# A new order for the seven products of the first matrix product, and one piece of operand work a step

## The chip, the cores and the metric

The kernel runs on one core of one Trainium2 chip, in one launch. A core has a matrix engine (TensorE, PE in the profile; its weight loads are PEld), a vector engine (VectorE, DVE), a scalar engine (ScalarE, ACT), a general engine (GpSimd, POOL) and the queue engine that issues the large transfers (SyncE, SP). Each engine runs its own list of instructions strictly in order and waits at an instruction until what it depends on is done. The metric is the time of one execution on the device in microseconds, and a kernel is told by the median of its runs.

## The reference

Three stages follow each other. Linear attention with a norm gives x of 2304 rows and 512 columns. A mixture of E = 4 dense experts, F = 1024 wide, follows, and then a soft mixture with 8 experts of 4 slots each. The change lies in the second stage:

```
kv  = einsum('bhsd,bhse->bhde', k, v);  out = einsum('bhsd,bhde->bhse', q, kv)
x   = out / sqrt(mean(out*out) + 1e-06) * g_norm        # 2304 x 512
p   = domain_probs / (domain_probs.sum(-1) + 1e-09)
for e in range(4):
    h    = maximum(x @ w1[e], 0)                         # 2304 x 1024, "first product"
    out += p[:, e:e+1] * (h @ w2[e])                     # 2304 x 512,  "second product"
# then: logits = x @ phi, softmax over tokens, slot inputs, 8 small experts, softmax over slots
```

## The kernel before, in words

**Numbers.** Every operand of the two products is kept as a pair of 16-bit numbers, hi (rounded) and lo (what is left), and each product is three matmuls: hi by hi, hi by lo, lo by hi, summed in the same accumulator bank.

**Tiling.** Tokens are cut into five chunks: 0 to 3 have 512 tokens, chunk 4 has 256. Chunks 0 and 1 form the first group, which runs experts 0, 1, 2, 3. Chunks 2, 3 and 4 form the second, which runs experts 3, 2, 1, 0. The first product of one expert and chunk is split into 2 by 2 blocks and done with seven block products P1 to P7 in place of eight (`PROD` names the operand blocks of each: blocks A11 to A22 of the tokens' side with sums S1 to S4, blocks B11 to B22 of the weights' side with sums T1 to T4). Each of them is done for u = 0 and u = 1, two halves of the columns. One such pair (P, u) is a **step**: 12 matmuls of 128x256 (128x128 in chunk 4), by line L890 in `mm1`. So a chunk's first product is 14 steps, in the order of `ORDER` (`ORDER2` in the fast form below): P for u = 0, P for u = 1, and then the next P.

**Banks.** For each u the products add up in three accumulator banks that the code calls x, y and z, and what is needed is a sum up to some point. In the plain form x takes P1, P6, P5, P3 in turn, y takes P2, and z takes P7 and P4. After P1, P6 and P5 the sum in x so far is copied out by ACT (L915); after P2 and P4 DVE adds the bank to such a copy (L918); after P5 it also adds z (L923). A product may not be added to a bank before the engine that reads its state so far is done; that order is kept by semaphores. x comes from a pool of two banks (one for each u), and y and z from another pool of two, so z of u = 0 takes the bank that y of u = 0 had.

**Plain form** (first group, expert 3 of the second group, and chunk 3 of the last expert). What comes out goes through `put`: ACT makes the relu and its hi (L906), and DVE makes lo (L907) one step later. The second product (`mm2`, L955) then reads h.

**Fast form** (experts 2, 1, 0 of the second group, apart from that last chunk). Here the second product is done with seven products too (`mm2_fast`, L991, in the order `ORDER3`), so that h's blocks and their sums S1 to S4 must be made as hi and lo pairs (`fast_h`). After each product ACT copies a bank out (L819 for P1, L821 for P6, L823 for P7), DVE adds a bank to a copy (L825 for P2, L829 for P5, L853 for P3), or ACT takes the relu of P4 (L833). The rest is done in pieces that wait in a list `todo`: the lo of a block (L802), a sum with its hi (L836 and L810 on DVE, with L797 on ACT), and the lo of a sum (L806). `work_off(2)` takes up to two pieces from the front of the list after each step of `mm1`, and `mm2_fast` takes one before each of its steps, or as many as it must until the block that it reads is made.

**Order.** For experts 2 and 1 the list of stages is first(2), first(3), second(2), first(4), second(3), second(4), numbers in brackets being chunks (`FASTSEQ`); for expert 0 it is first(2), first(4), second(2), first(3), second(4), second(3) (`LASTSEQ`). So one first product follows directly on another in one place for each of these three experts. Everything is written out in program order; background work (weights into hi and lo by L601 on ACT and L603 on DVE, sums of weights by L635 on POOL, attention of later chunks, the softmax of the third stage) is spread over the steps by `chain`. In the first chunk, hooks before steps 1, 3, 5, 7 and 9 make the operands that the next products need. For the second group, the weights' blocks of experts 2, 1, 0 are read back from memory in the order that `want_back` lists, on SP's queue.

## Time and profile before

| | |
|---|---|
| median of 3 runs | 870.9 us (870.34 to 871.3) |
| profiled execution | 870.41 us |
| its span, first to last instruction | 868.6 us |
| PE busy | 821.4 us, 95% of the span |
| DVE, ACT, POOL busy | 523.8, 350.6, 96.0 us |
| matmuls of the first product, L890 | 3360, 347.2 us |
| matmuls of the second product, L955 and L991 | 1104 and 1092, 246.1 and 121.0 us |
| mean granted clock of PE | 0.983 |

Each row of a timeline is one run of equal instructions: when it began, how long it took, engine and line, what it writes and reads, how many, and, in brackets, how long the engine had been idle just before and what ended that. "t <- p" means that tile t is written from tile p. Lines are those of the kernel before.

### The profile page before, as it was taken

The page shows a single profiled execution, that of the slowest core. Times are in us where ns is not written, and L with a number is a line of the kernel's source. Part 1 is how long each engine was busy: PE and PEld are TensorE (multiplying, and loading weights), DVE is VectorE, ACT ScalarE, POOL GpSimd, SP SyncE. Part 2 cuts the span into 40 slices and gives each one's busy share as a digit, 9 for nine tenths or more (in the row PEclk, how much of TensorE's full clock was granted, in tenths as well). Part 3 has the DMA queues.
Part 4 walks back from the last instruction along what each step waited for, and adds up shares of the span by engine and source line. Part 5 has one row for each costly group of instructions (what it writes and reads, how often), then busy time and mean ns, then how long its engine had stood idle before and what let it go on. Part 6 is the DMA issues. An engine that isn't in the chain of part 4 may idle for free.

```text
span 868.6 us, 16718 instructions
## 1 busy us (share of the span) xinstructions
PE 821.4 (95%) x7089; PEld 609.2 (70%) x7089; DVE 523.8 (60%) x1002; ACT 350.6 (40%) x681; POOL 96.0 (11%) x69
## 2 busy tenths in 40 slices
PE   8789899999999999999999998999899997999995
PEld 7575748575756676758485687898789887874444
DVE  4788898866895443755844348663876447452414
ACT  2675564553546232635552245222533044231213
POOL 2205622503150400000000000000000000000000
PEclk8799999999999999999999999999999999999998
DMA  8770500295129601125310110135004253079687
GB/s 337 298 267 25 212 31 1 76 356 223 68 86 402 246 1 50 68 79 196 118 54 1 53 46 1 36 136 194 2 1 171 81 204 124 6 268 400 218 350 219
DMA packets 40426, 123.86 MB, mean 143 GB/s; under 512 B 4256, under 2 KB 11296, under 8 KB 40352
## 3 DMA queue, kind: packets, MB, share of 16 engines
q1 hardware_dynamic: 39904, 122.70, 38.5%
q8 instruction: 55, 0.90, 0.4%
q14 instruction: 19, 0.16, 0.1%
q10 hardware_dynamic: 448, 0.10, 0.1%
HBM read 94.47 MB, written 28.31 MB: 141 GB/s over the span
## 4 chain that ended last, share of the span: by engine, by line
PE 68%; DVE 12%; ACT 6%; issue 1%; DMA 0%; SPq 0%; DVEq 0%; ACTq 0%
PE y L955 24%; PE p L890 22%; PE m L991 13%; DVE pages L603 2%; PE s L1578 2%; DVE pages L802 2%; ACT pages L795 1%; PE so L1616 1%; DVE pages L806 1%; PE o L335 1%; ACT t L915 1%; PE x2T L1020 1%; DVE t L810 1%; DVE t L825 1%; PE lg L1043 1%
## 5 line engine op out<-in xcount | busy, mean ns | idle before, releaser
L890 PE MATMUL p<-pages 128*128 128x256 f16 (+1 forms) x3360 | 347.2, 263 | 23.9 <-ACT pages L821 9.8
L890 PEld LDWEIGHTS <-pages 128*128 128x128 f16 x3360 | 302.5, 98 | 63.2 <-issue 29.2
L955 PE MATMUL y<-pages 128*128 128x512 f16 x1104 | 246.1, 379 | 2.5 <-DVE pages L964 2.0
L955 PEld LDWEIGHTS <-pages 128*128 128x128 f16 x1104 | 107.3, 98 | 125.8 <-issue 5.8
L991 PE MATMUL m<-pages 128*128 128x256 f16 x1092 | 121.0, 273 | 2.2 <-DVE pages L1001 2.2
L991 PEld LDWEIGHTS <-pages 128*128 128x128 f16 x1092 | 106.6, 98 | 15.8 <-issue 3.4
L603 DVE SCALAR_TENSOR_TENSOR pages<-pages,s_w 128x512 f16<-128x512 f32 x112 | 100.3, 938 | 5.4 <-ACT pages L601 5.4
L601 ACT ACTIVATE pages<-pages,s_w 128x512 f16<-128x512 f32 x112 | 73.5, 711 | 37.8 <-POOL pages L635 12.0
L915 ACT COPY t<-p 128x512 f32<-128x512 f32 (+1 forms) x72 | 40.0, 562 | 84.0 <-PE p L890 83.9
L906 ACT ACTIVATE pages<-t 128x512 f16<-128x512 f32 (+1 forms) x72 | 44.0, 612 | 71.5 <-DVE t L918 53.2
L1001 DVE SCALAR_TENSOR_TENSOR pages<-m,pc,pages 128x256 f32<-128x256 f32 x91 | 40.8, 481 | 40.7 <-PE m L991 40.6
L907 DVE SCALAR_TENSOR_TENSOR pages<-t,pages 128x512 f16<-128x512 f32 (+1 forms) x72 | 54.6, 761 | 3.0 <-ACT pages L906 0.6
L918 DVE TENSOR_TENSOR t<-p,t 128x512 f32<-128x512 f32 (+1 forms) x48 | 31.7, 664 | 35.2 <-PE p L890 35.2
L635 POOL TENSOR_TENSOR pages<-pages 128x1024 f32<-128x1024 f32 x16 | 40.3, 2521 | 96.6 <-DVE pages L603 62.8
L797 ACT CAST pages<-t 128x512 f16<-128x512 f32 (+1 forms) x48 | 25.5, 538 | 50.9 <-DVE t L810 39.6
L707 POOL TENSOR_TENSOR pages<-pages 128x512 f32<-128x512 f32 x24 | 35.6, 1484 | 81.2 <-DMA pages<-in_w 78.8
L966 DVE SCALAR_TENSOR_TENSOR pages<-y,pc,pages 128x512 f32<-128x512 f32 x28 | 21.0, 749 | 37.8 <-PE y L955 37.8
L1587 POOL MEMSET pages<- 128x1024 f32 x2 | 1.8, 951 | 374.8 <-PE s L1578 374.8
L923 DVE TENSOR_TENSOR t<-p,t 128x512 f32<-128x512 f32 (+1 forms) x24 | 16.1, 669 | 30.7 <-ACT t L915 30.6
L819 ACT COPY t<-p 128x512 f32<-128x512 f32 (+1 forms) x16 | 8.1, 505 | 57.7 <-PE p L890 57.7
L964 DVE TENSOR_SCALAR pages<-y,pc 128x512 f32<-128x512 f32 x18 | 13.4, 747 | 27.8 <-PE y L955 27.8
L795 ACT ACTIVATE pages<-pages 128x512 f16<-128x512 f32 (+1 forms) x32 | 17.2, 546 | 31.5 <-DVE pages L829 19.9
(188 smaller groups left out, 696.5 us busy)
## 6 DMA issues: line engine op xcount, KB each, us to landing
pages<-in_w SPq DMA_DIRECT2D x44, 512.0 KB, 7.9
o<-pages SPq DMA_DIRECT2D x33, 512.0 KB, 9.9
pages<-o SPq DMA_DIRECT2D x33, 512.0 KB, 4.4
pages<-in_m SPq DMA_DIRECT2D x32, 512.0 KB, 5.7
pages<-in_m2a SPq DMA_DIRECT2D x16, 512.0 KB, 6.6
pages<-in_m2b SPq DMA_DIRECT2D x16, 512.0 KB, 10.1
o_t<-pages SPq DMA_DIRECT2D x12, 512.0 KB, 2.8
pages<-o_t SPq DMA_DIRECT2D x12, 512.0 KB, 4.0
```

The costliest lines, as they stand in the source:

```text
L601: nc.scalar.activation(dst[:, 0], src, AF.Copy, scale=s)
L603: nc.vector.scalar_tensor_tensor(out=dst[:, 1], in0=src, scalar=s, in1=dst[:, 0], op0=ALU.mult, op1=ALU.subtract)
L635: self.eng.tensor_tensor(out=self.src(op).ap, in0=a.ap, in1=b.ap, op=ALU.subtract)
L707: eng.tensor_tensor(out=o, in0=a, in1=b, op=ALU.subtract)
L890: nc.tensor.matmul(ps[:, fp * n:fp * n + n], l, r, start=(fp + i == 0 and P in first), stop=(fp == 1 and i == len(mms) - 1 and P in end), ...
L906: nc.scalar.activation(hh, src, AF.Relu)
L907: late.append(lambda: nc.vector.scalar_tensor_tensor(out=hl, in0=src, scalar=0.0, in1=hh, op0=ALU.max, op1=ALU.subtract))
L915: nc.scalar.copy(t, ps)
L918: nc.vector.tensor_tensor(out=t, in0=ps, in1=t, op=ALU.add)
L955: nc.tensor.matmul(ps, a, b, start=(u + kk + fp + i == 0), stop=(u == 1 and kk == 1 and fp == 1 and i == 2))
L991: nc.tensor.matmul(ps, l, r, start=(i == 0 and j == 0 and P in (1, 2, 7)), stop=(i == len(mms) - 1 and j == nh - 1 and P in (2, 3, 4)), sk ...
L1001: nc.vector.scalar_tensor_tensor(out=x, in0=mbank[b][:, 256 * i:256 * i + 256], scalar=pcs[wk[1]][:, t:t + 1], in1=x, op0=ALU.mult, op1=AL ...
```

## The change

`ORDER2` goes, and `ORDER` holds for both forms: P1 P2 P6 P5 P7 P3 P4. The banks are the same in both forms now: x takes P1, P6, P7, P4; y takes P2; z takes P5 and P3. In the plain form P5 (alone in z) is copied by ACT, P7 and P3 are added by DVE, and P4 is the one that `put` reads directly from the bank; before it was P3. In `fast_h` P5 is copied by ACT, P7 and P3 are added by DVE and their hi is made at once (before, A12's hi came as a piece of work), P4's relu comes last, and S1 is made before S2. `work_off` after a step takes one piece, or two while more than 16 wait. The hooks of the first chunk split T1 before step 3 and the pages of T3 before step 5 (before, the other way round), and the read back order is B11, B21, T2, T1, T3, B22, T4.

```
-ORDER = (1, 2, 6, 7, 5, 3, 4)
-ORDER2 = (1, 2, 6, 7, 5, 4, 3)
+ORDER = (1, 2, 6, 5, 7, 3, 4)
...
-        for key in [("o1", o) for o in (B11, B21, T2, T3, T1, T4, B22)] + [
+        for key in [("o1", o) for o in (B11, B21, T2, T1, T3, B22, T4)] + [
...                                                          # fast_h
-        t6, t7, t4 = ([hraw(wk, c, op, v) for v in range(2)] for op in (S4, S1, A12))
+        t6, t5, t4 = ([hraw(wk, c, op, v) for v in range(2)] for op in (S4, S1, S2))
...
-        elif P == 7:
-            nc.scalar.copy(t7[u], ps)
+        elif P == 5:
+            nc.scalar.copy(t5[u], ps)
...
-        elif P == 5:
-            nc.vector.tensor_tensor(out=t7[u], in0=ps, in1=t7[u], op=ALU.add)
-            hi(u, A22, t7[u], True)
-            then(A22, lambda: lo(u, A22, t7[u], True))
-        elif P == 4:
+        elif P == 7:
+            nc.vector.tensor_tensor(out=t5[u], in0=ps, in1=t5[u], op=ALU.add)
+            hi(u, A22, t5[u], True)
+            then(A22, lambda: lo(u, A22, t5[u], True))
+        elif P == 3:
+            nc.vector.tensor_tensor(out=t6[u], in0=ps, in1=t6[u], op=ALU.add)
+            hi(u, A12, t6[u], True)
+            then(A12, lambda: lo(u, A12, t6[u], True))
+        else:
             nc.scalar.activation(t4[u], ps, AF.Relu)
...
+            def first(v, out, op1):
+                nc.vector.scalar_tensor_tensor(out=out[v], in0=t5[v], scalar=0.0, in1=out[v], op0=ALU.max, op1=op1)
...
                 for v in range(2):
-                    then(S2, lambda v=v: comb(v, S2, t1[v], t7[v], ALU.subtract))
+                    then(S1, lambda v=v: first(v, t4, ALU.add))
                 for v in range(2):
-                    then(S1, lambda v=v: comb(v, S1, t4[v], t7[v], ALU.add))
+                    then(S1, lambda v=v: (first(v, t1, ALU.subtract), hi(v, S1, t4[v], False)))
+                for v in range(2):
+                    then(S1, lambda v=v: (lo(v, S1, t4[v], False), hi(v, S2, t1[v], False)))
                 for v in range(2):
                     then(S2, lambda v=v: lo(v, S2, t1[v], False))
-                for v in range(2):
-                    then(S1, lambda v=v: lo(v, S1, t4[v], False))
...                                                          # mm1
-        if fast:
-            b = {1: "x", 6: "x", 7: "x", 4: "x", 2: "y", 5: "z", 3: "z"}[P]
-            first, end = (1, 2, 5), (2, 3, 4)
-        else:
-            b = {1: "x", 6: "x", 5: "x", 3: "x", 2: "y", 7: "z", 4: "z"}[P]
-            first, end = (1, 2, 7), (2, 3, 4)
+        b = {1: "x", 6: "x", 7: "x", 4: "x", 2: "y", 5: "z", 3: "z"}[P]
+        first, end = (1, 2, 5), (2, 3, 4)
...
-            work_off(2)
+            work_off(1 + (len(todo) > 16))
...
-        elif P in (2, 4):
-            t = d[1 if P == 2 else 6]
+        elif P == 4:
+            put(ps, 0, 1)
+        else:
+            t = d[{2: 1, 3: 6, 7: 5}[P]]
             nc.vector.tensor_tensor(out=t, in0=ps, in1=t, op=ALU.add)
-            put(t, 0, int(P == 4))
-        elif P == 3:
-            put(ps, 1, 0)
-        if P == 5:
-            nc.vector.tensor_tensor(out=d[5], in0=d["z"], in1=d[5], op=ALU.add)
-            put(d[5], 1, 1)
+            put(t, int(P != 2), int(P == 7))
...                                                          # hooks before steps 1, 3, 4, 5, 7, 9
-                             lambda: (x_split(2), w_split(T3)), lambda: [f() for f in kv1],
-                             lambda: (w_split(T1), w.t1.release()), lambda: w_split(B22),
+                             lambda: (w_split(T1), w.t1.release()), lambda: [f() for f in kv1],
+                             lambda: (x_split(2), w_split(T3)), lambda: w_split(B22),
```

How the instructions stand now is shown at three places. In these lists p1 is the bank x, p2 is y, p5 or p7 is z, and the numbers behind are group, expert, chunk and u. Lines of the changed kernel are 2 to 8 lower than those of the kernel before.

The first place is ACT in the plain form, chunk 0 of expert 1, from the copies of P6 to the last relu. Before:

```order
L915 COPY t6_0_1_0_0_1399<-p1_0_1_0_0_1321 128x512
L915 COPY t6_0_1_0_1_1415<-p1_0_1_0_1_1338 128x512
L915 COPY t5_0_1_0_0_1458<-p1_0_1_0_0_1321 128x512
L906 ACTIVATE pages_78<-t5_0_1_0_0_1458 128x2x256
L601 ACTIVATE pages_78<-pages_78,s_w2_0_544 128x512
L915 COPY t5_0_1_0_1_1480<-p1_0_1_0_1_1338 128x512
L906 ACTIVATE pages_78<-t5_0_1_0_1_1480 128x2x256
L601 ACTIVATE pages_78<-pages_78,s_w2_0_544 128x512
L906 ACTIVATE pages_78<-p1_0_1_0_0_1321 128x2x256
L906 ACTIVATE pages_78<-p1_0_1_0_1_1338 128x2x256
L906 ACTIVATE pages_78<-t6_0_1_0_0_1399 128x2x256
L906 ACTIVATE pages_78<-t6_0_1_0_1_1415 128x2x256
```

Now:

```order
L910 COPY t6_0_1_0_0_1399<-p1_0_1_0_0_1321 128x512
L910 COPY t6_0_1_0_1_1415<-p1_0_1_0_1_1338 128x512
L910 COPY t5_0_1_0_0_1431<-p5_0_1_0_0_1418 128x512
L910 COPY t5_0_1_0_1_1448<-p5_0_1_0_1_1435 128x512
L901 ACTIVATE pages_78<-t5_0_1_0_0_1431 128x2x256
L599 ACTIVATE pages_78<-pages_78,s_w2_0_548 128x512
L901 ACTIVATE pages_78<-t5_0_1_0_1_1448 128x2x256
L599 ACTIVATE pages_78<-pages_78,s_w2_0_548 128x512
L901 ACTIVATE pages_78<-t6_0_1_0_0_1399 128x2x256
L901 ACTIVATE pages_78<-t6_0_1_0_1_1415 128x2x256
L901 ACTIVATE pages_78<-p1_0_1_0_0_1321 128x2x256
L901 ACTIVATE pages_78<-p1_0_1_0_1_1338 128x2x256
```

The two copies of t5 read z and stand directly behind those of t6, ahead of any relu of t5; before, each read x and had a relu and a weight split (L601) ahead of the second. The relus that read a bank directly (p1) moved from the middle to the end.

The second place is DVE in the fast form, chunk 2 of expert 2, from the first sum for A22 on. Before:

```order
L829 TENSOR_TENSOR pages_78<-p5_1_2_2_0_5086,pages_78 128x512
L802 SCALAR_TENSOR_TENSOR pages_78<-pages_78 128x512
L829 TENSOR_TENSOR pages_78<-p5_1_2_2_1_5102,pages_78 128x512
L802 SCALAR_TENSOR_TENSOR pages_78<-pages_78 128x512
L836 SCALAR_TENSOR_TENSOR t1_1_2_2_0_4985<-t1_1_2_2_0_4985,pages_78 128x512
L836 SCALAR_TENSOR_TENSOR t1_1_2_2_1_5000<-t1_1_2_2_1_5000,pages_78 128x512
L806 TENSOR_TENSOR pages_78<-t1_1_2_2_0_4985,pages_78 128x512
L853 TENSOR_TENSOR pages_78<-p5_1_2_2_0_5086,pages_78 128x512
```

Now:

```order
L827 TENSOR_TENSOR pages_78<-p1_1_2_2_0_4972,pages_78 128x512
L800 SCALAR_TENSOR_TENSOR pages_78<-pages_78 128x512
L827 TENSOR_TENSOR pages_78<-p1_1_2_2_1_4987,pages_78 128x512
L800 SCALAR_TENSOR_TENSOR pages_78<-pages_78 128x512
L831 TENSOR_TENSOR pages_78<-p5_1_2_2_0_5060,pages_78 128x512
L800 SCALAR_TENSOR_TENSOR pages_78<-pages_78 128x512
L831 TENSOR_TENSOR pages_78<-p5_1_2_2_1_5074,pages_78 128x512
L800 SCALAR_TENSOR_TENSOR pages_78<-pages_78 128x512
L838 SCALAR_TENSOR_TENSOR t1_1_2_2_0_4985<-t1_1_2_2_0_4985,pages_78 128x512
L838 SCALAR_TENSOR_TENSOR t1_1_2_2_1_5000<-t1_1_2_2_1_5000,pages_78 128x512
L804 TENSOR_TENSOR pages_78<-t1_1_2_2_0_4985,pages_78 128x512
```

Before, the sums for A22 (L829) alternate with their lo (L802), and the sums for A12 (L853) come after the first sums for S3 (L836). Now the sums for A22 (L827) and those for A12 (L831) both alternate with the lo of the same block (L800), and the sums for S3 (L838) come behind all four.

The same chunk on ACT, from the copies of P6 to the first copies of the next chunk. Before:

```order
L821 COPY pages_78<-p1_1_2_2_0_4972 128x512
L821 COPY pages_78<-p1_1_2_2_1_4987 128x512
L823 COPY pages_78<-p1_1_2_2_0_4972 128x512
L823 COPY pages_78<-p1_1_2_2_1_4987 128x512
L795 ACTIVATE pages_78<-pages_78 128x512 x2
L833 ACTIVATE pages_78<-p1_1_2_2_0_4972 128x512
L797 CAST pages_78<-t1_1_2_2_0_4985 128x512
L833 ACTIVATE pages_78<-p1_1_2_2_1_4987 128x512
L797 CAST pages_78<-t1_1_2_2_1_5000 128x512
```

Now:

```order
L819 COPY pages_78<-p1_1_2_2_0_4972 128x512
L819 COPY pages_78<-p1_1_2_2_1_4987 128x512
L821 COPY pages_78<-p5_1_2_2_0_5060 128x512
L821 COPY pages_78<-p5_1_2_2_1_5074 128x512
L793 ACTIVATE pages_78<-pages_78 128x512 x4
L835 ACTIVATE pages_78<-p1_1_2_2_0_4972 128x512
L795 CAST pages_78<-t1_1_2_2_0_4985 128x512
L835 ACTIVATE pages_78<-p1_1_2_2_1_4987 128x512
L795 CAST pages_78<-t1_1_2_2_1_5000 128x512
L817 COPY t1_1_2_3_0_5191<-p1_1_2_3_0_5178 128x512
```

Before, two relus for hi (L795) stand ahead of P4's relus (L833) and two casts for S2 follow them. Now four stand ahead of P4's relus (L835), and the next chunk's copies of P1 (L817) follow one cast later.

The third place is DVE in the last expert, from the start of chunk 4's second product. Before:

```order
L1001 SCALAR_TENSOR_TENSOR pages_78<-m1_1_0_4_8221,pc_0_549,pages_78 128x256
L1158 TENSOR_REDUCE sc2_8237<-ce2_8127 128x4
L1159 TENSOR_SCALAR sc2_8237<-sc2_8237 128x4
L1160 RECIPROCAL sc2_8237<-sc2_8237 128x4
L1161 TENSOR_TENSOR ce2_8127<-ce2_8127,sc2_8237 128x128
L1001 SCALAR_TENSOR_TENSOR pages_78<-m7_1_0_4_8242,pc_0_549,pages_78 128x256
L1168 TENSOR_SCALAR c4_2_8256<-ce2_8127 128x4x32
L1169 SCALAR_TENSOR_TENSOR c4_2_8256<-ce2_8127,c4_2_8256 128x4x32
L1172 COPY c4_2_8256<-c4_2_8256 128x4x64
L1001 SCALAR_TENSOR_TENSOR pages_78<-m1_1_0_4_8221,pc_0_549,pages_78 128x256
L1127 SCALAR_TENSOR_TENSOR sacc_96<-sacc_96,al2_8107,sp2_8273 128x512
```

Now:

```order
L804 TENSOR_TENSOR pages_78<-pages_78 128x256
L993 SCALAR_TENSOR_TENSOR pages_78<-m1_1_0_4_8213,pc_0_553,pages_78 128x256
L1150 TENSOR_REDUCE sc2_8229<-ce2_8119 128x4
L1151 TENSOR_SCALAR sc2_8229<-sc2_8229 128x4
L1152 RECIPROCAL sc2_8229<-sc2_8229 128x4
L1153 TENSOR_TENSOR ce2_8119<-ce2_8119,sc2_8229 128x128
L804 TENSOR_TENSOR pages_78<-t1_1_0_4_0_7510,pages_78 128x256
L993 SCALAR_TENSOR_TENSOR pages_78<-m7_1_0_4_8235,pc_0_553,pages_78 128x256
L1160 TENSOR_SCALAR c4_2_8249<-ce2_8119 128x4x32
L1161 SCALAR_TENSOR_TENSOR c4_2_8249<-ce2_8119,c4_2_8249 128x4x32
L1164 COPY c4_2_8249<-c4_2_8249 128x4x64
L804 TENSOR_TENSOR pages_78<-t1_1_0_4_1_7531,pages_78 128x256
```

Seven pieces of chunk 4 are left in the list when its second product begins (three of them are the L804 here, two L808 and two L804 follow); before there were none.

## Rows read from the trace of the kernel before

**Rows 1.** Waits of PE, whole span: who waited for whom; us in total, times, longest.
```profile
PE p L890 <- ACT pages L821: 9.8, 8, 2.2
PE p L890 <- ACT t L915: 5.7, 6, 1.9
```

**Rows 2.** Timeline of PE, 50 to 150 us: start, us, line, count, [idle before].
```profile
56.82 1.47 PE L890 MATMUL p<-pages 128*128 128x256 f16 x12 [1.92 <-ACT t L915]
...
101.72 1.47 PE L890 MATMUL p<-pages 128*128 128x256 f16 x12 [1.41 <-ACT t L915]
104.19 4.09 PE L890 MATMUL p<-pages 128*128 128x256 f16 x36 [1.00 <-ACT t L915]
...
120.64 1.46 PE L955 MATMUL y<-pages 128*128 128x512 f16 x6 [2.00 <-DVE pages L964]
```

**Rows 3.** Timeline of DVE, 95 to 125 us.
```profile
101.70 0.69 DVE L923 TENSOR_TENSOR t<-p,t 128x512 f32<-128x512 f32 x1 [0.33 <-ACT t L915]
...
104.17 0.69 DVE L923 TENSOR_TENSOR t<-p,t 128x512 f32<-128x512 f32 x1 [1.12 <-ACT t L915]
...
119.84 0.74 DVE L964 TENSOR_SCALAR pages<-y,pc 128x512 f32<-128x512 f32 x1
```

**Rows 4.** Timeline of PE, 490 to 572 us (expert 2, second group).
```profile
499.24 23.95 PE L890 MATMUL p<-pages 128*128 128x256 f16 x216
523.50 2.78 PE L890 MATMUL p<-pages 128*128 128x256 f16 x24 [0.31 <-ACT t L819]
528.01 1.47 PE L890 MATMUL p<-pages 128*128 128x256 f16 x12 [1.73 <-ACT pages L821]
530.22 9.33 PE L890 MATMUL p<-pages 128*128 128x256 f16 x84 [0.75 <-ACT pages L821]
...
545.90 13.26 PE L991 MATMUL m<-pages 128*128 128x256 f16 x120 [1.11 <-DVE pages L1001]
...
563.71 5.52 PE L890 MATMUL p<-pages 128*128 128x128 f16 x96 [0.53 <-ACT pages L821]
```

**Rows 5.** Timeline of DVE and ACT, 509 to 517 us (chunk 2 of expert 2).
```profile
511.50 0.69 DVE L829 TENSOR_TENSOR pages<-p,pages 128x512 f32<-128x512 f32 x1 [4.00 <-PE p L890]
512.23 0.63 ACT L795 ACTIVATE pages<-pages 128x512 f16<-128x512 f32 x1 [1.52 <-DVE pages L829]
...
513.50 0.69 DVE L829 TENSOR_TENSOR pages<-p,pages 128x512 f32<-128x512 f32 x1
514.22 0.63 ACT L795 ACTIVATE pages<-pages 128x512 f16<-128x512 f32 x1 [1.36 <-DVE pages L829]
514.75 0.58 ACT L833 ACTIVATE pages<-p 128x512 f32<-128x512 f32 x1
```

**Rows 6.** Timeline of PE, 714 to 732 us (expert 0, second group).
```profile
715.77 0.83 PE L890 MATMUL p<-pages 128*128 128x128 f16 x12 [0.97 <-DVE pages L853]
717.95 1.62 PE L890 MATMUL p<-pages 128*128 128x128 f16 x24 [1.35 <-ACT t L819]
721.77 0.83 PE L890 MATMUL p<-pages 128*128 128x128 f16 x12 [2.19 <-ACT pages L821]
724.20 6.20 PE L890 MATMUL p<-pages 128*128 128x128 f16 x84 [1.60 <-ACT pages L821]
```

**Rows 7.** Busy time by stretch; the number ahead of the DMA share is PE's granted clock.
```profile
524.00:528.00 4.00, 2.28 (x21) 1.89 (x20) 3.98 (x8) 3.11 (x6) 0.00 (x0) 1.00 0.00 0
...
724.00:728.00 4.00, 3.80 (x45) 3.80 (x45) 1.76 (x5) 1.21 (x4) 0.00 (x0) 0.62 0.01 2
```

**Rows 8.** Timeline of all engines, 730 to 776 us.
```profile
736.46 0.41 DVE L806 TENSOR_TENSOR pages<-pages 128x256 f16<-128x256 f32 x1
...
766.07 0.69 DVE L923 TENSOR_TENSOR t<-p,t 128x512 f32<-128x512 f32 x1 [0.64 <-ACT t L915]
...
767.44 1.28 ACT L1082 ACT_TABLE_LOAD   x1
...
769.29 0.33 PE L1090 MATMUL dtr<-ident,dT 128*128 128x128 f32 x1 [1.73 <-ACT dT L1082]
```

More of the change, by code (lines that the diff above doesn't have):

```diff
@@ L843, in fast_h @@
                 for v in range(2):
-                    then(S2, lambda v=v: comb(v, S2, t1[v], t7[v], ALU.subtract))
+                    then(S1, lambda v=v: first(v, t4, ALU.add))
                 for v in range(2):
-                    then(S1, lambda v=v: comb(v, S1, t4[v], t7[v], ALU.add))
+                    then(S1, lambda v=v: (first(v, t1, ALU.subtract), hi(v, S1, t4[v], False)))
+                for v in range(2):
+                    then(S1, lambda v=v: (lo(v, S1, t4[v], False), hi(v, S2, t1[v], False)))
                 for v in range(2):
                     then(S2, lambda v=v: lo(v, S2, t1[v], False))
-                for v in range(2):
-                    then(S1, lambda v=v: lo(v, S1, t4[v], False))
-        else:
-            nc.vector.tensor_tensor(out=t6[u], in0=ps, in1=t6[u], op=ALU.add)
-            if u == 1:
-                then(A12, lambda: [hi(v, A12, t6[v], True) for v in range(2)])
-                for v in range(2):
-                    then(A12, lambda v=v: lo(v, A12, t6[v], True))
                 for v in range(2):
@@ L872, in mm1 @@
         d = us[u]
-        if fast:
-            b = {1: "x", 6: "x", 7: "x", 4: "x", 2: "y", 5: "z", 3: "z"}[P]
-            first, end = (1, 2, 5), (2, 3, 4)
-        else:
-            b = {1: "x", 6: "x", 5: "x", 3: "x", 2: "y", 7: "z", 4: "z"}[P]
-            first, end = (1, 2, 7), (2, 3, 4)
+        b = {1: "x", 6: "x", 7: "x", 4: "x", 2: "y", 5: "z", 3: "z"}[P]
+        first, end = (1, 2, 5), (2, 3, 4)
         if P in first:
@@ L1252, in attn_moe_softmoe_kernel @@
                     st = [lambda wk=wk, c=c, u=u, P=P, fast=fast: mm1(wk, c, u, P, fast)
-                          for P in (ORDER2 if fast else ORDER) for u in range(2)]
+                          for P in ORDER for u in range(2)]
                     if not fast:
```

## The prediction

> **What bounds the kernel now.** The table of busy time comes first: PE is busy 821.4 of 868.6 us, so at most 47 us are to be had, and only where PE waits. The view of PE's waits names for whom: on L890, the first product, it waits 9.8 us for L821 and 5.7 us for L915 [rows 1]. Both are ACT's copies of a bank's state so far. The timeline of PE then shows where. In the plain form a gap stands before P3 (56.82, 101.72, 104.19 [rows 2]): P3 goes into x, which P5 has just filled, and ACT has one step to copy it. In the fast form the gaps before P7 (528.01, 530.22, 563.71 [rows 4]; 721.77, 724.20 [rows 6]) are the same for P6 and P7. A step is 23.95 us / 18 = 1.33 us [rows 4]; in chunk 4 it is 5.52 / 8 = 0.69 us. Last I read DVE and ACT in order of time, to see why a copy of 0.6 us isn't done in 1.33 us: they feed each other. A sum by DVE at 511.50 lets ACT make hi at 512.23, and only behind the lo of that block comes DVE's next sum, 513.50, so a product with such a pair costs these two engines 2.0 us a step and falls back 0.67 us behind PE [rows 5]. Lateness collects there, and PE pays for it where a bank is used again soon.
>
> **The change part by part.** The number of matmuls, copies, sums, relus and pieces is the same, so nothing is won but waits. In the new order a bank that has been read is written again three steps later (P6 to P7, P5 to P3, P7 to P4), about 4.0 us in place of 1.33, within one first product.
>
> *Plain form.* All six waits on L915, 5.7 us, lose their cause, since P5's copy has three steps. What of it reaches the end is less. Two of them (1.41 and 1.00) are followed by a wait of 2.00 at 120.64 for L964 [rows 2], and between them DVE works through one queue that ends with L964 at 119.84. That queue stood still 0.33 and 1.12 us for the copies of P5 [rows 3]; these go, so L964 comes 1.5 us earlier, and PE gets 1.5 of its 2.4 us and gives the rest back at L964. Bounds: 0 and 2.4. The first wait, 1.92, lies in the start, where DVE and ACT split weights without pause and the second product waits for them next; no row decides, so I take the middle of 0 and 1.9, 1.0. The other three, 5.7 - 1.92 - 2.41 = 1.4, stand alone and count in full. P3's lo now needs a sum first, but it is wanted only after P4's two steps and the first unit of L955. Sum: 3.9 us.
>
> *Fast form, experts 2 and 1.* They repeat each other. In each, PE waits 0.31 before P6 (for P1's copy), 1.73 and 0.75 before P7, all in chunk 3, whose first product follows directly on that of chunk 2; then 1.11 for DVE in the second product; then 0.53 before P7 in chunk 4 [rows 4]. That is 4.43 us, 8.9 for both. With one piece a step DVE has at most two operations of 0.6 to 0.7 us in a step of 1.33 us, so I let all five go.
>
> *What comes in their place.* At the seam of two first products the old neighbourhood comes back: P4, the last, is in x, and the next chunk's P1 takes the same two banks of x after one step. So P1 of u = 0 waits for P4's relu of u = 0 (L833), and ahead of this relu on ACT stand four relus for hi, as the rows of the new order show. Worked out with rows 5: P7's sum stands where P5's stood, at 511.50. Four pairs at 2.0 us put P3's second sum at 517.50. Its hi on ACT starts 0.73 later, at 518.23, and the relu of P4 0.53 after that start (514.22 to 514.75), 518.76, and ends at 519.34. P4's last matmul ends at 499.24 + 14 x 1.33 = 517.87. PE waits 1.47. One more link of DVE (sum for S3, 0.7) and ACT (its hi) puts the relu of u = 1 at the end at 521.35, while P1 of u = 0 ends at 520.69: 0.66 more. That is 2.1 us a seam, 4.2 for the two experts; behind the waiting matmul all of PE's list stands. Bounds: 0, if ACT comes early enough, and twice this. Net 8.9 - 4.2 = 4.7 us.
>
> *Fast form, expert 0.* Chunk 4 follows chunk 2, with steps of 0.69 us. The waits of 0.97, 1.35, 2.19 and 1.60 are 6.1 us [rows 6]. The 84 matmuls behind them take 6.20 us where 84/96 x 5.52 = 4.83 is usual: 1.4 us for a granted clock of 0.62 in 724 to 728, a mix of the levels of 1.2 and 2.4 GHz, while it stayed 1.00 behind the smaller waits at 524 to 528 [rows 7]. Both go. The seam costs 1.47, and then, as P1's narrow step ends at 520.05 on the scale above, 1.30; and DVE, which has 14 wide pieces (0.6 us apart) and six narrow sums (0.4) in fourteen steps, 10.8 against 9.7 us, lets PE wait more at P3: 0 to 1.1, I take 0.4, since the seam itself gives DVE time. That is 3.2, and 7.5 - 3.2 = 4.3 us.
>
> The Trainium skill (TensorE: Matmul & The Clock Gate, "A second HAM failure mode: psum-queue depth-cycling") says that a PE which pauses again and again as it cycles through banks also pays for clock that is taken back. The trace agrees after the larger waits and not after the smaller ones [rows 7]. By the rule each seam could cost a further 1.4 us, the price of rows 6; the sum would then lose up to 4.2 us.
>
> *End of expert 0.* The slower pace leaves seven pieces of chunk 4 to its second product. They are narrow (0.41 us on DVE [rows 8]) but stand between the small softmax operations, and P6 there needs two of them: I count six such operations, three to each half of P6, less what P1 and P7 hide, 1.3 us; bounds 0 and 2.6. Against it, the softmax's exponential: PE waits 1.73 for it at 769.29, behind a table load at 767.44, behind the chain of P5's second copy and sum at 766.07 [rows 8]. That sum reads a copy that is two steps older now, so the 0.64 that DVE stood still and the copy itself, some 0.6, leave the chain: 1.2 us. Together -0.1 us.
>
> *The rest.* The exchanged hooks and the exchanged read back of T1 and T3 cost nothing: each still stands before its product by as much as its predecessor did, and no wait of L890 for a transfer is in the view of waits. If this cover failed, it would show as such a wait.
>
> Sum: 3.9 + 4.7 + 4.3 - 0.1 = 12.8 us. The profiled execution took 870.41 us, 1.8 us of it outside the span; that gives 857.6, and with the median of the runs 0.5 us above that execution, 858 us.
>
> **The rivals.** *No wait at the seam.* If ACT reaches P4's relu in time, because hi and lo don't wait for each other as in rows 5, the 4.2 and 3.2 us stay won: 858 - 7.4 = about 851. For it: P3 is done two steps ahead of the seam. Against it: in DVE's new list each sum stands behind the lo of the sum before it, as in rows 5, and nothing overtakes in a list.
>
> *A worse seam.* Each seam also takes the clock, 3 x 1.4 = 4.2, and the start gives back the 1.0 that I count: 863; or each costs twice as much, 858 + 7.4 = 865. For it: in rows 6 and 7 waits of this size did take the clock. Against it: at 528 they did not. The rule of the Trainium skill that is named above speaks for this case.
>
> *Slower: three steps are too few.* The waits come from how late ACT is, not from who is next to whom: at 523.50 P6 waited though P1 was four steps back, and in expert 0 this cost 1.35 [rows 4, 6]. The copy that PE awaited at 528.01 was there 1.73 + 1.33 = 3.1 us after its product had ended; the new distance covers 4.0. If the four pairs before the seam and the wider spread of the pieces make ACT one step later than that in the next chunk, 5.3 us, PE waits 1.33 us before P7 and then goes at the pairs' pace of 2.0 us for the six steps of P7, P3 and P4: 1.33 + 6 x 0.67 = 5.4 us at each of three seams, 858 + 16 = 874. It decides from 4.0 us of lateness on, and turns to a loss at about 5. Against it speaks that in that chunk a sum is followed by an older piece and not by its own lo, so DVE has at most 1.3 us of work in a step of 1.33 us.
>
> *It doesn't do what it says.* Where DVE's queue is the bound, as at 120.64, PE gets back none of the waits that go; with that everywhere in the plain form, and the pieces at the end at 2.6, it would be 858 + 3.9 + 1.3 = 863.
>
> **How the numbers follow.** The forecast has 0.53, and its own range is 854 to 862; no wait at the seam 0.14, the worse seam 0.16, the queue of DVE 0.05, slower or level by lateness 0.12. The range for 8 in 10 runs from 851.5, where half of the first rival is left out, to 866, which takes in the second. 0.2% of 870.9 is 1.7 us, about what a measurement can tell. Lateness of 4 to 5 us is level, beyond it slower, half each: faster 0.88, same 0.06, slower 0.06.
>
> **What would show it.** In the waits of PE the rows for the copy of P6 and for the plain copies should be gone or under 1 us each. A new row must stand there, L890 waiting for P4's relu, 6 times and about 6 to 7 us, all at the three seams. DVE's wait at 104.17 is gone, and that of PE for L964 is longer than 2.00. The mean clock in the stretch after expert 0's seam is 1.00. The wait at the exponential falls to about 0.5. The forecast is wrong if P7, P3 or P4 wait inside a first product, if second products wait for lo pieces in experts 2 and 1, or if L890's new waits pass 10 us.

## The result, and the profile after

The changed kernel takes **856.7 us** (median of 4 runs, 856.25 to 858.82), against 871.1 us for the kernel before on the same chip (4 runs, 870.34 to 872.56). The ratio is 0.9838, 95% interval 0.9817 to 0.9858. Its profiled execution has a span of 855.0 us, 13.6 less than before. The work is the same. PE's idle time fell by 9.7 us, from 47.2 to 37.5: ahead of L885, the first product (L890 before), it is 11.8 us, where it was 23.9 in the page of before, while ahead of L947, the plain second product (L955 before), it grew from 2.5 to 5.8. The other 3.9 us are busy time, 817.5 in place of 821.4 us, at a mean granted clock of 0.986 in place of 0.983. The groups of the page after (busy, mean of one in ns | idle just before and what ended most of it):

```profile
L885 PE MATMUL p<-pages 128*128 128x256 f16 (+1 forms) x3360 | 342.6, 262 | 11.8 <-ACT pages L835 6.4
...
L947 PE MATMUL y<-pages 128*128 128x512 f16 x1104 | 248.4, 381 | 5.8 <-DVE pages L902 1.9 <-DVE pages L601 1.9 <-ACT pages L901 1.8
...
L983 PE MATMUL m<-pages 128*128 128x256 f16 x1092 | 121.0, 273 | 1.2 <-DVE pages L804 1.2
```

PE's waits after the change (in total, times, longest), which answer to [rows 1]. The copy of P6 and the plain copies, 9.8 and 5.7 us, are gone. P4's relu (L835) has come, and three rows of waits in the plain second product (L947).

```profile
PE p L885 <- ACT pages L835: 6.4, 6, 1.4
...
PE y L947 <- DVE pages L902: 1.9, 1, 1.9
PE y L947 <- DVE pages L601: 1.9, 3, 1.1
PE y L947 <- ACT pages L901: 1.8, 1, 1.8
...
PE m L983 <- DVE pages L804: 1.2, 2, 0.6
...
PE dtr L1082 <- ACT dT L1074: 0.7, 1, 0.7
```

The same in order of time, PE: the first group's second products (answer to [rows 2]), expert 2 ([rows 4]), expert 0 ([rows 6]), the end ([rows 8]).

```profile
62.34 0.81 PE L947 MATMUL y<-pages 128*128 128x512 f16 x3 [1.05 <-DVE pages L601]
...
108.15 0.60 PE L947 MATMUL y<-pages 128*128 128x512 f16 x2 [1.82 <-ACT pages L901]
110.68 11.79 PE L947 MATMUL y<-pages 128*128 128x512 f16 x46 [1.93 <-DVE pages L902]
...
516.65 1.47 PE L885 MATMUL p<-pages 128*128 128x256 f16 x12 [1.42 <-ACT pages L835]
518.64 17.19 PE L885 MATMUL p<-pages 128*128 128x256 f16 x156 [0.52 <-ACT pages L835]
...
704.98 0.83 PE L885 MATMUL p<-pages 128*128 128x128 f16 x12 [1.41 <-ACT pages L835]
706.98 9.19 PE L885 MATMUL p<-pages 128*128 128x128 f16 x154 [1.16 <-ACT pages L835]
...
754.01 0.33 PE L1082 MATMUL dtr<-ident,dT 128*128 128x128 f32 x1 [0.70 <-ACT dT L1074]
...
760.38 0.83 PE L983 MATMUL m<-pages 128*128 128x256 f16 x6 [0.57 <-DVE pages L804]
```

DVE's two pauses of [rows 3] are gone, and its list reaches L956 (L964 before) 1.2 us earlier. But a split of weights (L601) and only then P3's sum (L915) stand at 105 to 107 us, and from 106.33 us on PE waits for that sum's relu:

```profile
105.08 1.75 DVE L601 SCALAR_TENSOR_TENSOR pages<-pages,s_w 128x512 f16<-128x512 f32 x1
106.75 0.68 DVE L915 TENSOR_TENSOR t<-p,t 128x512 f32<-128x512 f32 x1
...
118.62 0.75 DVE L956 TENSOR_SCALAR pages<-y,pc 128x512 f32<-128x512 f32 x1 [1.15 <-PE y L947]
```

Why P4's relu is late stands in DVE's and ACT's rows, chunk 2 of expert 2. DVE makes a sum (L827, L831), waits 0.70 for ACT's hi, makes the lo (L800), and only then the next sum: 1.99 us from sum to sum, as in [rows 5]. The relu at 516.02 stands behind the last hi.

```profile
508.79 0.69 DVE L827 TENSOR_TENSOR pages<-p,pages 128x512 f32<-128x512 f32 x1 [3.79 <-PE p L885]
510.18 0.69 DVE L800 SCALAR_TENSOR_TENSOR pages<-pages 128x512 f16<-128x512 f32 x1 [0.70 <-ACT pages L793]
510.79 0.68 DVE L827 TENSOR_TENSOR pages<-p,pages 128x512 f32<-128x512 f32 x1
...
515.48 0.63 ACT L793 ACTIVATE pages<-pages 128x512 f16<-128x512 f32 x1 [1.36 <-DVE pages L831]
516.02 0.58 ACT L835 ACTIVATE pages<-p 128x512 f32<-128x512 f32 x1
```

The same sums in chunk 3, where pieces of chunk 2 are still in the list, begin 1.31 us apart: an older piece stands where the sum's own lo stood, and DVE waits for nothing.

```profile
529.39 0.69 DVE L827 TENSOR_TENSOR pages<-p,pages 128x512 f32<-128x512 f32 x1 [2.17 <-PE p L885]
530.00 0.68 DVE L804 TENSOR_TENSOR pages<-t,pages 128x512 f16<-128x512 f32 x1
530.70 0.69 DVE L827 TENSOR_TENSOR pages<-p,pages 128x512 f32<-128x512 f32 x1
```

From the start of a stage's first matmul to the start of the next stage's, in PE's timelines, the parts of the prediction measure as follows. In brackets is how the stages were before and after, each in one profiled execution.

| part | predicted gain | measured |
|---|---|---|
| plain form, up to expert 2 (499.24 and 496.73) | 3.9 | 2.5 |
| experts 2 and 1 (194.67 and 188.34) | 4.7 | 6.3 |
| expert 0, first(2) and first(4) (36.32 and 31.05) | 4.3 | 5.3 |
| from there to the end (138.39 and 138.86) | -0.1 | -0.5 |
| sum | 12.8 | 13.6 |

### The profile page after: what moved, and what is told of

It is laid out like the page before. It is cut to its first block, busy times and chain, and to the rows that moved or that the text cites. A ratio compares the mean times of both kernels' runs of the same rounds, so it can differ in the third digit from the quotient of the medians.

```text
span 855.0 us, 16733 instructions
## 1 busy us (share of the span) xinstructions
PE 817.5 (96%) x7089; PEld 606.5 (71%) x7089; DVE 524.0 (61%) x1002; ACT 350.9 (41%) x681; POOL 95.6 (11%) x69
## 4 chain that ended last, share of the span: by engine, by line
PE 82%; DVE 8%; ACT 3%; POOL 2%; DMA 2%; issue 2%; SPq 0%; DVEq 0%; POOLq 0%
PE p L885 30%; PE y L947 26%; PE m L983 14%; DVE pages L601 2%; PE o L333 2%; PE so L1608 2%; PE s L1570 1%; PE kv L278 1%; DVE pages L800 1%; PE xT L402 1%; DVE t L915 1%; PE x2T L1012 1%; DMA pages<-in_w 1%; DMA pages<-in_v 1%; ACT pages L793 1%
## 5 line engine op out<-in xcount | busy, mean ns | idle before, releaser
L885 PE MATMUL p<-pages 128*128 128x256 f16 (+1 forms) x3360 | 342.6, 262 | 11.8 <-ACT pages L835 6.4
L885 PEld LDWEIGHTS <-pages 128*128 128x128 f16 x3360 | 300.5, 98 | 48.2 <-issue 14.5
L947 PE MATMUL y<-pages 128*128 128x512 f16 x1104 | 248.4, 381 | 5.8 <-DVE pages L902 1.9
L947 PEld LDWEIGHTS <-pages 128*128 128x128 f16 x1104 | 107.5, 98 | 131.3 <-issue 8.2
L601 DVE SCALAR_TENSOR_TENSOR pages<-pages,s_w 128x512 f16<-128x512 f32 x112 | 97.5, 911 | 7.3 <-ACT pages L599 7.2
L915 DVE TENSOR_TENSOR t<-p,t 128x512 f32<-128x512 f32 (+1 forms) x72 | 47.7, 665 | 51.6 <-PE p L885 48.0
L901 ACT ACTIVATE pages<-t 128x512 f16<-128x512 f32 (+1 forms) x72 | 43.9, 611 | 64.8 <-DVE t L915 64.2
L910 ACT COPY t<-p 128x512 f32<-128x512 f32 (+1 forms) x72 | 39.9, 565 | 68.0 <-PE p L885 67.8
L993 DVE SCALAR_TENSOR_TENSOR pages<-m,pc,pages 128x256 f32<-128x256 f32 x91 | 40.8, 480 | 41.6 <-PE m L983 41.4
L902 DVE SCALAR_TENSOR_TENSOR pages<-t,pages 128x512 f16<-128x512 f32 (+1 forms) x72 | 57.1, 797 | 9.8 <-ACT pages L901 8.5
L795 ACT CAST pages<-t 128x512 f16<-128x512 f32 (+1 forms) x48 | 25.7, 539 | 49.1 <-DVE t L838 28.1
L956 DVE TENSOR_SCALAR pages<-y,pc 128x512 f32<-128x512 f32 x18 | 13.5, 748 | 31.7 <-PE y L947 31.7
L804 DVE TENSOR_TENSOR pages<-t,pages 128x512 f16<-128x512 f32 (+1 forms) x48 | 28.1, 585 | 1.1
L800 DVE SCALAR_TENSOR_TENSOR pages<-pages 128x512 f16<-128x512 f32 (+1 forms) x32 | 18.5, 587 | 8.7 <-ACT pages L793 8.5
```

Source lines behind the costliest of these rows:

```text
L601: nc.vector.scalar_tensor_tensor(out=dst[:, 1], in0=src, scalar=s, in1=dst[:, 0], op0=ALU.mult, op1=ALU.subtract)
L885: nc.tensor.matmul(ps[:, fp * n:fp * n + n], l, r, start=(fp + i == 0 and P in first), stop=(fp == 1 and i == len(mms) - 1 and P in end), ...
L901: nc.scalar.activation(hh, src, AF.Relu)
L902: late.append(lambda: nc.vector.scalar_tensor_tensor(out=hl, in0=src, scalar=0.0, in1=hh, op0=ALU.max, op1=ALU.subtract))
L910: nc.scalar.copy(t, ps)
L915: nc.vector.tensor_tensor(out=t, in0=ps, in1=t, op=ALU.add)
```

## The experiments

Two theories stood at the beginning: the new order pays, since a bank is used again three steps later, or the slower pace pays, since DVE and ACT are no longer late. Times are medians; the intervals are those of the ratio to the kernel before, 871.05 to 871.28 us on those chips.

**e1_pace_only**, the kernel before with the new pace alone:

```
-            work_off(2)
+            work_off(1 + (len(todo) > 16))
```

> The kernel before with its own two orders, and only the pace of the pieces changed: one piece after a step of a fast first product, two while more than 16 wait. Theory A (bank distance): the waits come from a bank that is written again one step after it was filled; that stays, so most of the waits before P7 stay, and of the 11.6 us that the fast stages gave back (3.16 + 3.16 + 5.27) at most 3 appear: 868 to 871 us. Theory B (lateness): the waits come from ACT and DVE being late behind the pairs and pieces; one piece a step takes the lateness away and the copies fit in one step, so 8 us or more appear: at or under 863 us.

Measured: 858.2 us (0.9838 to 0.9864), as theory B has it. With both old orders, nearly the whole gain is there. Of the eight waits for P6's copy, 9.8 us, three are left, 4.1 us:

```profile
PE p L890 <- ACT t L915: 5.4, 6, 1.6
PE p L890 <- ACT pages L821: 4.1, 3, 1.7
```

They lie in chunk 4, the one of narrow steps. In expert 2 a wide piece of 0.62 us from the chunk before stands there on ACT ahead of the copy:

```profile
559.38 0.62 ACT L797 CAST pages<-t 128x512 f16<-128x512 f32 x1 [0.24 <-DVE t L810]
559.90 0.37 ACT L821 COPY pages<-p 128x256 f32<-128x256 f32 x1
```

**e2_order_only**, the changed kernel with `work_off(2)`:

> The changed kernel with two pieces after each step, as before. Theory A (bank distance): the distance of three steps, about 4.0 us, covers the lateness of 3.1 us that two pieces a step make, so nearly all of the gain stays: 856 to 859 us. Theory B (lateness): DVE and ACT fall back as before, P4's relu at the three seams comes later and the waits before P7 come back in part: 861 us or more.

Measured: 873.2 us (1.0001 to 1.0025), so no gain and, if anything, a loss. Theory A falls by its number. In experts 2 and 1 its mechanism holds inside the first product: first(2) and first(3) take 38.94 us, as in the changed kernel. But two pieces a step empty the list, so DVE and ACT now take turns in chunk 3 too. The sums' pieces come late, and the second product waits for its own evictions (L993), which are queued behind them:

```profile
537.25 0.68 DVE L831 TENSOR_TENSOR pages<-p,pages 128x512 f32<-128x512 f32 x1
538.62 0.69 DVE L800 SCALAR_TENSOR_TENSOR pages<-pages 128x512 f16<-128x512 f32 x1 [0.70 <-ACT pages L793]
539.23 0.68 DVE L831 TENSOR_TENSOR pages<-p,pages 128x512 f32<-128x512 f32 x1
```
```profile
546.60 14.82 PE L983 MATMUL m<-pages 128*128 128x256 f16 x120 [3.23 <-DVE pages L993]
```

In expert 0 the mechanism fails inside the first product too. Behind the seam PE waits for the sum of P2 ahead of P5 (L823, 1.4 us) and then for the copy of P6 ahead of P7, although three steps lie between these two; the first products take 35.33 in place of 31.05 us:

```profile
726.88 0.83 PE L885 MATMUL p<-pages 128*128 128x128 f16 x12 [0.69 <-ACT pages L819]
728.86 3.08 PE L885 MATMUL p<-pages 128*128 128x128 f16 x48 [1.15 <-ACT pages L819]
```

**e3_plain_only**, the kernel before with the new order, banks and hooks in the plain form alone (`ORDER`, and the plain branch of `mm1`, as in the change):

> The new order in the plain form alone; the fast form keeps its old order, banks, pieces and pace. By the prediction's term for the plain form: 3.9 us less and the softmax's 1.2, 866 us. By the stages of the two traces: PE stands 2.5 us earlier where expert 2 of the second group begins, and gains 1.15 in the last chunk's plain product: 867.5 us. A rival by which the plain form gives nothing (DVE's queue is the bound everywhere): 870 to 871 us.

Measured: 869.5 us (0.9957 to 0.9982), 1.8 less than before. By the median the prediction's 5.1 for this edit was too much. But single runs lie from 865.3 to 870.2, and the fastest, which is the one with a trace, has the whole of it: its span is 5.1 us shorter than that of before (863.5), and its expert 2 begins 3.9 us earlier (495.31). In this execution the granted clock stayed at 1.00 behind the new waits of the second product; the last section tells how often it did not.

**e4_seam_banks**, the changed kernel with other banks where one first product follows directly on another:

```
-            d[b] = (ps_x if P == 1 else ps_yz)(f"p{P}_{nm}")[:, :2 * n]
+            seam = fast and c == (4 if wk[1] == 0 else 3)
+            d[b] = (ps_x if (P == 1) != seam else ps_yz)(f"p{P}_{nm}")[:, :2 * n]
```

> The changed kernel, where the first product that follows directly on another takes its banks the other way round (P1 from the pool of y and z, P2 and P5 from the pool of x), so that P1 does not wait for P4's relu. If the wait at the seam is the bank alone, all of it goes: 6.4 us by the view of waits, and about 0.16 for each restart, six of them: 849 to 850 us. If ACT and DVE are late at the seam whatever the bank, the wait turns up at P6 or P7 of the next chunk (for P1's or P6's copy), and less than 3 us are gained: 854 to 857 us.

Measured: 853.1 us (0.9781 to 0.9811), between the two. In experts 2 and 1 the seam is gone whole: 38.94 becomes 36.87, 2.1 us each. In expert 0 nothing is won (31.05 and 31.04). There P2 is the next to write P4's banks, behind P1's narrow steps, and waits for the same late relu; then P6 waits for P1's copy (L817) and P7 for P6's (L819), as the second expectation had it:

```profile
703.00 0.83 PE L886 MATMUL p<-pages 128*128 128x128 f16 x12 [1.16 <-ACT pages L835]
704.64 3.51 PE L886 MATMUL p<-pages 128*128 128x128 f16 x60 [0.82 <-ACT t L817]
708.54 3.75 PE L886 MATMUL p<-pages 128*128 128x128 f16 x60 [0.39 <-ACT pages L819]
```

**e7_keep_one**, which takes away the turn-taking itself:

```
-            work_off(1 + (len(todo) > 16))
+            work_off(min(1 + (len(todo) > 16), len(todo) - 1))
```

> The changed kernel, where work_off always leaves the newest piece in the list, so that no lo is taken right behind its own sum. Theory A (in the chunk before a seam the list is empty, each lo stands behind its own sum and DVE waits 0.70 for the hi from ACT, two engines at 2.0 us a step): the pairs run at 1.33, P4's relu is in time and the seams' 6.4 us and restarts go to a large part: 850 to 853 us. Theory B (the wait at the seam is ACT's four relus ahead of P4's, and the bank): nothing changes there: 856 to 858 us.

Measured: **851.3 us** (0.9756 to 0.9787), as theory A has it. All six waits at the seams are gone: first(2) and first(3) take 36.68 us, 28 steps of 1.31, and expert 0's pair 27.89 in place of 31.05. DVE's list in chunk 2 is now as it was in chunk 3: a sum, then an older piece, first the lo of P2's block (from t), then that of the sum before:

```profile
511.44 0.69 DVE L827 TENSOR_TENSOR pages<-p,pages 128x512 f32<-128x512 f32 x1 [5.26 <-PE p L885]
512.04 0.68 DVE L800 SCALAR_TENSOR_TENSOR pages<-t,pages 128x512 f16<-128x512 f32 x1
512.75 0.69 DVE L827 TENSOR_TENSOR pages<-p,pages 128x512 f32<-128x512 f32 x1
513.35 0.68 DVE L800 SCALAR_TENSOR_TENSOR pages<-pages 128x512 f16<-128x512 f32 x1
```

**e8_before_keep_one**, the kernel before with `work_off(min(2, len(todo) - 1))`:

> The kernel before with two pieces a step, but the newest piece always left in the list. Theory A (lateness comes from overload: a sum and two pieces are 1.8 us and more of DVE in a step of 1.33 us): that stays, and most of the waits before P7 stay: 867 to 871 us. Theory B (lateness comes from DVE and ACT waiting for each other in turn, 2.0 us a step): that goes, and with it most of what one piece a step gave (13 us): 858 to 862 us.

Measured: 864.5 us (0.9910 to 0.9937), between the two theories: in the old order, keeping the newest piece alone brings 6.6 us, about half of the 13 that one piece a step brings (e1). So taking turns accounts for about half, and two pieces beside a sum in one step for the rest.

**e10_old_order_one_keep**, the kernel before with one piece and the newest kept:

> The kernel before with its own orders and banks; one piece a step, and the newest stays in the list. Theory A (the fast form's waits are lateness alone, so that once it is gone the order of the products is worth nothing there): only the plain form's gain is missing against the changed kernel with the newest piece kept (851.3): 853.5 to 855.5 us. Theory B (bank distance still counts): the waits for P6's copy stay in chunk 4 and expert 0, as with one piece a step alone (1.2, 1.2 and 1.7 us): 857 us or more.

Measured: 858.7 us (0.9843 to 0.9873), no better than one piece alone, as theory B has it. With the turn-taking gone, ACT is still late beside the narrow steps of 0.67 us, behind wide pieces of 0.62 us, and the copy of P6 one step before P7 costs 1.2 us in chunk 4 and 1.7 in expert 0, as in e1:

```profile
559.99 5.64 PE L890 MATMUL p<-pages 128*128 128x128 f16 x96 [1.21 <-ACT pages L821]
...
711.09 5.52 PE L890 MATMUL p<-pages 128*128 128x128 f16 x96 [1.69 <-ACT pages L821]
```

**e12_new_order_two_keep**, the changed kernel with `work_off(min(2, len(todo) - 1))`:

> The changed kernel with two pieces a step, and the newest always left in the list. Theory A (turn-taking of DVE and ACT is one cause, overload by two pieces the other, and three steps between the uses of a bank cover the overload): no wait at the seams, second products that no longer wait for DVE, 851 to 853 us. Theory B (with two pieces a step the overload alone keeps DVE late): 860 us or more.

Measured: 851.3 us (0.9757 to 0.9796), as theory A has it. In the new order two pieces a step do no harm in experts 2 and 1 once the newest is kept. In expert 0, where narrow steps follow, they cost 3.9 us (31.75 in place of 27.89), and in the last stage 2.4 come back (from its second product to the end 96.40 in place of 98.82); its median is level with e7's, with runs from 849.4 to 854.3 us. Now the eight cases stand side by side, with two stages from their profiles. The medians with the new order hold the plain form's new order too, worth 2 to 3 us (e3, e11); the stages don't.

| order, pieces a step | median us | expert 2: first(2) to the end of first(4) | expert 0: first(2), first(4) |
|---|---|---|---|
| old, two (before) | 871.1 | 69.83 | 36.32 |
| old, one (e1) | 858.2 | 66.28 | 30.66 |
| old, two, newest kept (e8) | 864.5 | 67.09 | 35.87 |
| old, one, newest kept (e10) | 858.7 | 66.07 | 29.89 |
| new, two (e2) | 873.2 | 71.61 | 35.33 |
| new, one (the change) | 856.7 | 66.66 | 31.05 |
| new, two, newest kept (e12) | 851.3 | 64.40 | 31.75 |
| new, one, newest kept (e7) | 851.3 | 64.40 | 27.89 |

The new order, its banks and the order of the pieces in `fast_h` came together, and no run takes these apart. What speaks for the banks is e7 in chunk 4 of expert 2. There 14 even steps of 0.67 us begin at 554.40, so that P6 of u = 1 ends at 558.42. Its copy ends 1.7 us later, at 560.16: too late for a P7 that follows after one step, and in time for one that follows after three, at 560.43.

```profile
559.79 0.37 ACT L819 COPY pages<-p 128x256 f32<-128x256 f32 x1
```

**e5_units**, the changed kernel with another order of units in one plain second product (chunk 1 of expert 0, first group). A unit is six matmuls that read one half of h, kk = 0 or 1; for the first two token tiles all kk = 0 units now come first, then those of kk = 1, which read what P3 makes.

> The changed kernel; only in chunk 1 of expert 0 in the first group the second product takes the four units that read the kk = 0 half of h for its first two token tiles ahead of the four that read kk = 1, so that P3's operand is needed about 4 us later (three units of 1.3 us). Theory A (P3's relu and lo are late behind DVE's list, and the two waits of 1.82 and 1.93 then take the clock): both waits and most of the 1.7 us of the clock go, this stage takes 22 in place of 26.7 us, 851 to 853 us in all. Theory B (DVE's list is the bound of this stretch, as the prediction had it): PE meets the next result of DVE as late as before and gains under 1.5 us: 855 to 857 us.

Measured: 857.6 us (0.9832 to 0.9859), no gain, as theory B has it. The stage takes 25.67 in place of 26.73 us, which shows little, since without this edit it took from 24.80 (e12) to 27.84 us (e7) in other profiles. The waits of 1.82 and 1.93 become 0.21 and one of 2.20 for L956, the end of a DVE queue that works from 102 to 120 almost without pause; behind this one wait the granted clock fell to 0.65 in 120 to 124 us. So here the prediction's view, DVE as the bound, was right, and its 1.5 us was not.

```profile
120.08 1.67 PE L947 MATMUL y<-pages 128*128 128x512 f16 x6 [2.20 <-DVE pages L956]
```

**e6_pieces**, the changed kernel with `work_off(1)` after each step of the last chunk's plain product:

> The changed kernel, with one piece of the list also taken after each step of the plain first product of the last chunk, so that the seven pieces left from chunk 4 are done before its second product. If the pieces cost 1.3 us as the prediction says (0.57 and 0.62 waited and two restarts of about 0.16): 855.2 us, the last stage 96.5 in place of 98.2 us. Rival: the pieces then stand between the sums and the softmax's small operations of that stretch, and the wait for the exponential grows by as much: 856 to 857 us.

Measured: 855.7 us (0.9809 to 0.9841); the interval overlaps that of the changed kernel, so the time alone shows nothing. The stage does: from the last second product's first matmul to the end of the span it takes 96.43 in place of 98.18 us, and the plain product before it is unchanged at 22.34.

**e9_keep_and_pieces**, e7 and e6 together:

> The changed kernel with both edits that helped: the newest piece stays in the list, and each step of the last chunk's plain product takes one piece too. If they add up, 851.3 less the 1.75 us that the last stage gave and the 0.65 that it lost with the newest piece kept: 849 us. Rival: the pieces kept longer meet the softmax's small operations, and only the first gain stays: 851 us.

Measured: **849.3 us** (ratio 0.9740, interval 0.9722 to 0.9759), faster than both kernels. The two edits add up: the last stage takes 96.36 us here, 98.82 in e7.

**e11_old_plain**, e9 with the old order, banks and hooks in the plain form:

> The changed kernel with both edits that helped, and in the plain form alone the old order P1 P2 P6 P7 P5 P3 P4 with its old banks and hooks. The difference to the same kernel with the new order is the plain form's worth: 3.9 and 1.2 us by the prediction (854 us), 2.5 and 1.15 by the stages of the two traces (852.5 us), 0 to 1 if DVE's list is the bound (849 to 850 us).

Measured: 851.8 us (0.9766 to 0.9793). The plain form's new order is worth 2.6 us here, end of the kernel included, and 1.8 in e3. The middle one of the three expectations comes nearest.

## Why the prediction was right, and where it was not

The time, 858 against 856.7, lies well inside its range. But that it came so near was in part luck: errors of its terms cancel, and the cause it named for the largest terms was half of the truth.

*Plain form, 3.9 us: too large; measured 2.5 (and 3.9 in e3's profile, where the clock stayed).* The waits on L915 are gone as forecast. The start gave 0.5 in place of 1.0: PE stood 2.5 us earlier when the second product began, and gave 2.0 back, most of it in waits for L601. And 0.8 us of the lead were there at P6 already (43.52 in place of 44.31), at a granted clock of 0.86 in place of 0.80 in 20 to 45 us, so that the new order itself gave nothing here. Chunk 1 of expert 0 was to give 1.5 and cost 0.9. The step that failed is "PE gets 1.5 of its 2.4 us and gives the rest back at L964": DVE's L964 (L956 now) did come 1.2 us earlier, but PE waited before it, for P3's h (L901, L902). The sum that P3's lo needs was "wanted only after P4's two steps and the first unit"; DVE's queue was later than that. So the sign "that of PE for L964 is longer than 2.00" failed: PE has no wait for L956 at all. And after the two waits the clock was lost for a while:

```profile
112.00:116.00 4.00, 4.00 (x14) 1.51 (x13) 4.00 (x7) 3.97 (x7) 1.43 (x1) 0.67 0.00 0
```

This took 1.7 us (46 matmuls in 11.79 us, 10.10 in e12), a term that the sum did not have; e3 and e12, where the clock stayed, gained 0.8 and 1.1 in chunk 1. The rest of the plain form gave 2.9 in place of 1.4: 1.9 by the three waits with their restarts (next paragraph), and 1.0 in amounts of under 0.3 us a stage for which no row of PE's waits stands.

*Restart.* Part of that is a term that was missing. A wait costs PE more than the row shows: the wait of 1.11 before L991 took 1.27 us out of its stage when it went (19.61 and 18.34), that of 0.53 took 0.69 (10.07 and 9.38). So 0.16 us a wait, five waits less two in each of experts 2 and 1, gives 0.5 us of the 0.8 by which each beat its forecast of 2.35; another 0.2 is the seam, 1.94 in place of 2.13.

*Fast form: right in size, wrong in cause.* The step that failed is "In the new order a bank that has been read is written again three steps later", taken as what removes the waits. The new order without the new pace gains nothing (e2), and the pace without the order gains nearly all (e1). The "about 4.0 us" that three steps cover is also true of wide steps alone: in chunk 4 they are some 2.0, and in e2's expert 0 P7 waited behind them. On top of the pace the order is worth 1.5 us in the medians, no more than the plain form's share; in the fast form it moves PE's wait from P7 in chunk 4 to the seam (66.28 and 66.66 us in the table). Only with the newest piece kept does the new order pay clearly: in expert 2 66.07 becomes 64.40 with one piece a step and 67.09 becomes 64.40 with two; in expert 0 29.89 becomes 27.89 with one and 35.87 becomes 31.75 with two. What the new pace takes away, a third operation of DVE beside its "two operations of 0.6 to 0.7 us in a step", stood as a side remark, and no rival split the change there. "The waits come from how late ACT is, not from who is next to whom" was argued in the rival on the slower side, and e2 shows its price of 2.0 us a step.

*The seam: right.* Predicted 1.47 and 0.66, measured 1.42 and 0.52; in expert 0 1.47 and 1.30, measured 1.41 and 1.16. The six waits are 6.4 us, as the sign had it (6 to 7). The reason holds as well: e7 removes DVE's stand behind ACT and the seams vanish. ACT's four hi were late, not too many: in e7 they stand ahead of the relu as well.

*Expert 0.* Predicted 4.3, measured 5.3. The waits removed, 6.1, with four restarts (0.6) and the clock (1.4), less the seam's two (2.6 and 0.3), give 5.2. The 0.4 taken for DVE's narrow sums did not come. The clock is 1.00 after the seam:

```profile
704.00:708.00 4.00, 1.85 (x31) 1.73 (x31) 2.34 (x4) 2.36 (x5) 0.00 (x0) 1.00 0.94 373
```

*The end.* The exponential's wait fell from 1.73 to 0.70, and the stage before won 1.15 (1.2 forecast). The seven pieces cost 1.6 (1.3 forecast): two waits of 0.57 and 0.62, and their restarts. e6 confirms it by taking them away.

*Hooks and read back.* No wait of L885 for a transfer stands in the view after, as forecast; these two were not tried apart, and neither were the two pieces a step that the new pace allows while more than 16 wait.

## What to carry to other kernels

When one engine makes hi and another subtracts it to make lo, try not to put the lo right behind its own sum: with one older piece between, both engines ran at the pace of their work here (1.31 in place of 1.99 us from sum to sum). Before a wait on a copy is put down to a bank that comes back too soon, look at whether the copying engine was late. If it was, pace the background work first and reorder afterwards: here either hid what the other was worth. When a change has two parts, forecast each alone.

## What was not expected of the hardware

The same instructions with nearly the same waits take different times. In chunk 1 of expert 0 the changed kernel's second product waits about 1.8 us twice with 0.60 us of work between. What follows, 46 matmuls, took 10.10 us in one execution (e12) and 13.00 in another (e7), and the granted clock accounts for the difference. First PE's row of e12 and of e7, then the stretch 112 to 116 us of each, where the clock is 1.00 and 0.50, the upper and the lower of its two levels:

```profile
110.57 10.10 PE L947 MATMUL y<-pages 128*128 128x512 f16 x46 [1.69 <-DVE pages L902]
```
```profile
112.10 13.00 PE L947 MATMUL y<-pages 128*128 128x512 f16 x46 [1.83 <-DVE pages L902]
```
```profile
112.00:116.00 4.00, 4.00 (x21) 1.79 (x19) 4.00 (x8) 3.97 (x7) 1.33 (x1) 1.00 0.00 0
```
```profile
112.00:116.00 4.00, 3.90 (x10) 1.42 (x11) 4.00 (x6) 4.00 (x7) 2.77 (x2) 0.50 0.00 0
```

Of the eight profiles with these two waits (after, e2, e3, e4, e6, e7, e9, e12) two kept the clock at 1.00 in 112 to 116 us (e3, e12); the others show 0.50 to 0.67 there. In e2, e6 and e9 it fell already in 64 to 68 us, to 0.62 to 0.68, behind the waits for L601. So in the new plain order the start of the next expert's first product lies anywhere from 129.8 (e12) to 134.2 us (e7; 3.0 of these 4.4 us arise in this stage, the others before it), and from 131.2 to 131.9 in the five profiles with the old one (before, e1, e8, e10, e11). That is the likely source of the spread in e3's runs, of which only one has a trace. What tips the clock in one execution and not in another the traces don't show. The Trainium skill (TensorE: Matmul & The Clock Gate, "A second HAM failure mode: psum-queue depth-cycling") speaks of clock lost to short idle times between groups of matmuls. The trace agrees in e7's execution, and not in e12's, nor at the changed kernel's seams, where 1.41 and 1.16 us with a step of 0.83 between left the clock at 1.00.
